# Splitting the first batch's x on GpSimd, another order of the first loads, and g_norm's column on ScalarE's queue

## The chip, the cores and the metric

The kernel runs on one core of one Trainium2 chip. The metric is device time in microseconds (us), the median of several executions. A core has five engines with queues of their own: TensorE (PE in the profile; PEld are its weight loads), VectorE (DVE), ScalarE (ACT), GpSimd (POOL) and SyncE (SP). SP does no arithmetic here and issues most of the transfers; ACT and POOL can issue transfers too. All transfers run on the same 16 DMA engines.

## The reference

Three stages in a row, all in float32. The first is a linear attention without softmax over 8 batches of 576 tokens with 8 heads of 64, followed by a root-mean-square norm with a gain. The other two are two-layer networks with 4608 tokens, 512 features and 2048 hidden units.

```
kv  = einsum('bhsd,bhse->bhde', k, v)
out = einsum('bhsd,bhde->bhse', q, kv)
x   = out / sqrt(mean(out*out, -1) + 1e-6) * g_norm      # to [4608, 512]
h   = x @ w_in;   r = max(h, 0);  x = (r*r) @ w_out      # moe
h   = x @ w_in2;  out = (h*cos(h)) @ w_out2              # moe2
```

## The kernel before, in words

The matmuls of the two networks run in a rounded 32-bit format. Each operand is therefore split into a high part (a cast to the rounded format) and a low part (the operand less the high part), and a product is three matmuls: high by high, high by low, low by high. The weights arrive in 64-bit floating point and are converted on DVE and ACT from integer words (`words` and `value`, L107 to L127; L205 and L206 split the result).

The program has two parts. In the first, the attention and half of the first network's work run interleaved: tokens go in tiles of 512 (`TOK`), hidden units in chunks of 128. `run_chunks` (L811) walks over (tile, chunk) pairs; between the matmuls of a chunk it calls `run_jobs`, which carries out a list of small jobs sorted by a position n counted in chunks. The attention of the eight batches, the conversions of weights and the reloads of x are such jobs. Everything with a position of -1 or less is emitted ahead of the first chunk. In the second part, from 424 us on, the rest of both networks runs as products of seven block matmuls (`run_slots`).

The attention of one batch b works in units (b, p, i): p is one of four column blocks of 128 features (two heads), i one of two halves. First `kv_mm` (L250) multiplies keys and values in five blocks of up to 128 tokens, the fifth of 64, and ACT copies the result into kvx (L272). `att_a` (L279) multiplies a block of queries by it (L289); ACT squares the result into sq (L300) and scales it by gcol, the column of g_norm, into og (L301). `att_b` sums the squares on PE (L315) and takes the reciprocal root on ACT (L320, L322). `att_c` refines it with three DVE operations, L330 to L332, of which the last writes xo; xo has three buffers. For batches 0 and 1, `att_d` splits xo directly into the operands xh and xl of the first two tiles: a cast on ACT (L349) and a subtraction on DVE (L350). Batch 0 gives eight units and, as the first tile ends within the second half of its tokens, twelve pieces: per column block one of 288 columns, one of 224 and one of 64. `att_e` stores xo to DRAM on POOL's queue (L356). `layer_in` (L371) then multiplies x by the first weights; its first two chunks run side by side and walk over the four column blocks in order (L380).

The order of the loads is that in which the program calls them on SP's queue. `load_w` (L151) loads a weight block of 512 KB and `load_kv` (L247) a block of keys and values of 512 KB (256 KB the fifth), `load_q` (L276) a block of queries of 288 KB. Two streams, `w_stream` and `kv_stream`, hold the order within each kind, and `advance` issues the next ones. Ahead of the first jobs the program loads the two halves of g_norm's column, weight blocks one and two, five blocks of keys and values, weight blocks three and four, and three blocks of queries; the fourth is loaded when the first block's buffer is free. Conversions are emitted in the order of the weight blocks.

The order of instructions on each engine isn't just the order of the program. A planner goes over them at build time with modelled durations and puts ready instructions first, so that, for instance, ACT's copies into kvx stand ahead of conversions that the program emits earlier. Waits between engines are set by it as well.

Of the kernel before, what the change touches and what calls it, by code (L numbers as in the profile page):

```python
# [13 lines left out]
ALU = mybir.AluOpType  # L14
# [8 lines left out]
def kernel(  # L23
# [15 lines left out]
    nc = tc.nc  # L39
# [7 lines left out]
    NRAW = 4  # L47
    KVB = 5
# [3 lines left out]
    D = 64  # L52
# [16 lines left out]
    gcol = cpool.tile([P, 1], F32, name="gcol")  # L69
# [26 lines left out]
    def as32(ap):  # L96
        return ap.bitcast(F32)
# [114 lines left out]
    def new_x(t, c):  # L212
        more = dict(bufs=2) if t == 1 and c > 1 else {}
        xs[t, c] = [x_p.tile([P, TOK], F32R, tag=n + "2" * len(more), name=n, **more) for n in ("xh", "xl")]
        return xs[t, c]
# [119 lines left out]
    def att_d(*u):  # L335
        b, p, hf = u
        xo = att[u]
        if b >= NEXACT:
            return
        tok = b * S + hf * HS  # L340
        for t in range(NDIRECT):
            lo, hi = max(tok, t * TOK), min(tok + HS, (t + 1) * TOK)
            if lo >= hi:
                continue
            if (t, p) not in xs:
                new_x(t, p)
            h, l = (x[:, lo - t * TOK:hi - t * TOK] for x in xs[t, p])
            piece = xo[:, lo - tok:hi - tok]
            nc.scalar.copy(out=h, in_=piece)  # L349
            nc.vector.tensor_tensor(out=l, in0=piece, in1=as32(h), op=ALU.subtract)  # L350

    def att_e(*u):
        b, p, i = u
# [381 lines left out]
    w_stream = Stream(load_w, conv_w, w_items)  # L735
# [4 lines left out]
    kv_stream = Stream(load_kv, kv_mm, [(b, c) for b in range(B) for c in range(NSC)])  # L740
# [126 lines left out]
        run_jobs(here)  # L867

    for j in range(2):
        nc.sync.dma_start(out=gcol[j * D:(j + 1) * D, :], in_=g_norm.rearrange("(d o) -> d o", o=1))  # L870
    nc.vector.memset(epsb, EPS)
    nc.scalar.activation(out=zerob, in_=epsb, func=AF.Abs_reciprocal_sqrt)
    nc.vector.memset(zerob, 0.0)
# [1 line left out]
    nc.vector.memset(as32(ones[:]), 0.0)  # L875
    for j in range(2):
        nc.vector.memset(as32(ones[j * D:(j + 1) * D, j * D:(j + 1) * D]), 1.0)
    nc.vector.tensor_scalar(out=gcol, in0=gcol, scalar1=-0.5 / D, scalar2=None, op0=ALU.mult)

    with ExitStack() as early:  # L880
        pools["ps"] = early.enter_context(tc.tile_pool(name="ps0", bufs=1, space=PSUM))
        def right(name, bufs):
            return early.enter_context(tc.tile_pool(name=name, bufs=bufs, side="right"))

        right("pad", 1).tile([P, 56], F32, name="pad")
        ev_p, pools["raw"] = right("ev", 2), right("conv", 2)
        x_p, g_p, pools["t"] = (right(n, b) for n, b in (("x", XB), ("g", 3), ("tmp", 8)))
        with tc.tile_pool(name="att", bufs=1, side="right") as att_p:
            kvx = [att_p.tile([P, NKC, P], F32, tag=f"kvx{b}", name=f"kvx{b}") for b in range(2)]
            for x in kvx:  # L890
                nc.gpsimd.memset(x, 0.0)
            w_stream.advance(2)
            kv_stream.advance(KVB)
            w_stream.advance(NRAW - 2)
            for p in range(NQ):
                load_q(0, p)
            run_jobs(-1)
            banks.update(o=["o", "l1"], ss=["ss"], l=["l0", "acc3"])
            run_chunks(0, nAtt)
        pools["x"] = ctx.enter_context(tc.tile_pool(name="xb", bufs=13, side="left", reuse_waits="tile"))  # L900
        banks["l"] = ["l0", "l1", "o", "ss"]
        run_chunks(nAtt, nA0)
        for c in chunks[-LAG:]:
            layer_out(*c)
# [48 lines left out]
```

## Time and profile before

| | |
|---|---|
| Median of 3 runs | 1560.13 us (1560.1 to 1560.59) |
| The profiled execution's own time | 1560.23 us |
| Its span, from first to last instruction | 1558.5 us |
| PE busy (matmuls) | 1532.7 us |
| DVE busy | 1294.7 us |
| ACT busy | 1076.2 us |
| POOL busy | 108.6 us |
| Moved by DMA | 426.71 MB, mean 274 GB/s |

Times in the profile count from the first instruction of the program. Some 1.7 us of the execution's own time lie around the span. An engine counts as busy while one of its instructions runs; issuing a transfer doesn't count on SP. In a row of the timeline the number in brackets is how long the engine was idle before the instruction, with what ended the idleness. A `q` behind an engine's name stands for its queue's sequencer.

### The profile page before, as it was taken

The page shows a single profiled execution, that of the slowest core. Times are in us where ns is not written, and L with a number is a line of the kernel's source. Part 1 is how long each engine was busy: PE and PEld are TensorE (multiplying, and loading weights), DVE is VectorE, ACT ScalarE, POOL GpSimd, SP SyncE. Part 2 cuts the span into 40 slices and gives each one's busy share as a digit, 9 for nine tenths or more (in the row PEclk, how much of TensorE's full clock was granted, in tenths as well). Part 3 has the DMA queues.
Part 4 walks back from the last instruction along what each step waited for, and adds up shares of the span by engine and source line. Part 5 has one row for each costly group of instructions (what it writes and reads, how often), then busy time and mean ns, then how long its engine had stood idle before and what let it go on. Part 6 is the DMA issues. An engine that isn't in the chain of part 4 may idle for free.

```text
span 1558.5 us, 24657 instructions
## 1 busy us (share of the span) xinstructions
PE 1532.7 (98%) x9104; PEld 1346.8 (86%) x9104; DVE 1294.7 (83%) x1744; ACT 1076.2 (69%) x1529; POOL 108.6 (7%) x172
## 2 busy tenths in 40 slices
PE   5999999999999999999999999999999999999998
PEld 3777777778888888888998899999999999999998
DVE  7987888888886899989889979867986788779777
ACT  5977777775444765656556777776777677777775
POOL 1112111110000000000000000000000000000001
PEclk9999999999999999999999999999999999999999
DMA  9848998777678979898999788887888789899996
GB/s 322 281 148 240 284 284 268 229 214 214 202 230 296 327 246 375 294 382 268 364 340 372 261 281 253 257 280 214 256 248 283 214 246 275 290 336 293 298 314 170
DMA packets 222295, 426.71 MB, mean 274 GB/s; under 512 B 18016, under 2 KB 138080, under 8 KB 222176
## 3 DMA queue, kind: packets, MB, share of 16 engines
q1 hardware_dynamic: 210560, 390.13, 73.4%
q0 software_dynamic: 11616, 35.01, 10.5%
q8 instruction: 73, 1.20, 0.3%
q14 instruction: 46, 0.38, 0.1%
HBM read 317.72 MB, written 81.79 MB: 256 GB/s over the span
## 4 chain that ended last, share of the span: by engine, by line
PE 88%; DMA 4%; DVE 4%; issue 2%; ACT 1%; SPq 0%; POOL 0%; DVEq 0%; ACTq 0%; POOLq 0%
PE FB L506 15%; PE FA L506 15%; PE SA L639 15%; PE SB L639 15%; PE acc L417 12%; PE l L380 10%; DMA ws<-ws_d 1%; PE o L380 1%; PE ss L380 1%; DMA xraw<-x_d 1%; DMA q<-in_qT 1%; DMA sum<-part 1%; DMA wi<-wi_d 1%; PE l L259 1%; DVE gl L616 0%
## 5 line engine op out<-in xcount | busy, mean ns | idle before, releaser
L506 PE MATMUL FA<-xh,wi 128*128 128x512 f32 (+1 forms) x840 | 301.4, 370 | 0.0
L506 PE MATMUL FB<-xh,wi 128*128 128x512 f32 (+1 forms) x840 | 301.4, 370 | 0.0
L639 PE MATMUL SA<-ws,gh 128*128 128x256 f32 x1008 | 233.2, 280 | 0.4 <-issue 0.4
L639 PE MATMUL SB<-ws,gh 128*128 128x256 f32 x1008 | 233.0, 280 | 0.5 <-ACT part L664 0.5
L639 PEld LDWEIGHTS SA<-ws,gh 128*128 128x128 f32 x1008 | 183.7, 188 | 13.0 <-ACT y L558 0.7
L639 PEld LDWEIGHTS SB<-ws,gh 128*128 128x128 f32 x1008 | 183.3, 188 | 12.4 <-ACT part L664 0.7
L506 PEld LDWEIGHTS FB<-xh,wi 128*128 128x128 f32 x840 | 157.2, 188 | 9.4
L506 PEld LDWEIGHTS FA<-xh,wi 128*128 128x128 f32 x840 | 157.1, 188 | 9.0
L639 PE MATMUL SB<-ws,gl 128*128 128x256 f32 x504 | 141.2, 280 | 0.3 <-DVE gl L616 0.3
L639 PE MATMUL SA<-ws,gl 128*128 128x256 f32 x504 | 141.2, 280 | 0.1
L616 DVE TENSOR_TENSOR gl<-y,gh 128x1024 fp32r<-128x1024 f32 (+1 forms) x98 | 109.5, 1117 | 36.5 <-ACT gh L615 36.4
L576 DVE SCALAR_TENSOR_TENSOR y<-y,h 128x1024 f32<-128x1024 f32 (+1 forms) x79 | 88.2, 1117 | 46.2 <-ACT y L572 45.9
L665 POOL DMA_DIRECT2D sum<-part x54 | 46.5, 862 | 1136.3 <-DMA wi_d<-raw 530.3
L558 ACT ACTIVATE y<-h,zerob 128x1024 int32<-128x1024 f32 (+1 forms) x79 | 84.1, 1064 | 49.1 <-DVE h L532 48.5
L417 PE MATMUL acc<-gh,wh 128*128 128x512 f32 x288 | 113.6, 396 | 0.0
L417 PE MATMUL acc<-gl,wh 128*128 128x512 f32 x288 | 112.9, 392 | 0.0
L417 PE MATMUL acc<-gh,wl 128*128 128x512 f32 x288 | 112.6, 391 | 0.0
L506 PE MATMUL FA<-xl,wi 128*128 128x512 f32 (+1 forms) x300 | 110.9, 370 | 0.0
L506 PE MATMUL FB<-xl,wi 128*128 128x512 f32 (+1 forms) x300 | 110.9, 370 | 0.0
L568 ACT ACTIVATE y<-y 128x1024 f32<-128x1024 f32 (+1 forms) x79 | 77.2, 978 | 36.0 <-DVE y L562 36.0
L639 PE MATMUL SA<-gh,ws 128*128 128x512 f32 (+1 forms) x280 | 100.8, 369 | 1.1 <-DMA ws<-ws_d 0.6
L639 PE MATMUL SB<-gh,ws 128*128 128x512 f32 (+1 forms) x280 | 100.6, 369 | 0.1
(181 smaller groups left out, 3816.6 us busy)
## 6 DMA issues: line engine op xcount, KB each, us to landing
wi<-wi_d SPq DMA_DIRECT2D x210, 512.0 KB, 6.6
ws<-ws_d SPq DMA_DIRECT2D x210, 512.0 KB, 5.5
sum<-part POOLq DMA_DIRECT2D x33, 512.0 KB, 7.3
kvld<-in_kv SPq DMA_DIRECT2D x32, 512.0 KB, 6.7
ws_d<-raw SPq DMA_DIRECT2D x24, 448.0 KB, 4.3
q<-in_qT SPq DMA_DIRECT2D x32, 288.0 KB, 4.4
p_d<-ev SPq DMA_DIRECT2D x18, 512.0 KB, 3.7
raw<-in_wA SPq DMA_DIRECT2D x16, 512.0 KB, 6.0
```

What stands on the lines that cost most here:

```text
L259: nc.tensor.matmul(kv_ps[b][r, p, r], t[:n, 0, head], t[:n, 1, head], start=(c == 0 and p == 0), stop=(c == NSC - 1), skip_group_check=True,)
L380: nc.tensor.matmul(ps, a[:, 0, cs], m[:], start=(c == 0 and k == 0), stop=(c == NKC - 1 and k == 2))
L417: nc.tensor.matmul(o, a[:, cs], m[:], start=(f == 0 and n == 0), stop=(f == NH - 1 and n == 2), skip_group_check=True)
L506: nc.tensor.matmul(ps[:, pp, :], a, b, start=(n == 0 and (i in (0, 2) or i == 1 and not seeded(k))), stop=(n == 5), skip_group_check=True,)
L558: nc.scalar.activation(out=y.bitcast(I32), in_=hs[k, b], func=AF.Identity, bias=zerob)
L568: nc.scalar.activation(out=y, in_=y, func=AF.Sin, scale=math.pi)
L576: nc.vector.scalar_tensor_tensor(out=y, in0=y, scalar=-2.0 * math.pi, in1=hs.pop((k, b)), op0=ALU.add, op1=ALU.mult)
L616: nc.vector.tensor_tensor(out=l, in0=src, in1=as32(h), op=ALU.subtract)
L639: nc.tensor.matmul(ps[:, b, :], lhs, rhs, start=(n == 0 and (m == 0 or b % 2 == 0) and i in (0, 1, 2)), stop=(n == 5), skip_group_check=True,)
L665: nc.gpsimd.dma_start(out=e, in_=part, accum_op=ALU.add)
```

## The change

Three edits. The split of batch 0's xo runs on POOL, cast and subtraction; that of batch 1 stays on ACT and DVE. The two loads of g_norm's column are issued on ACT's queue instead of SP's, and its scaling runs on POOL instead of DVE. The third weight block is loaded behind three of the five blocks of keys and values instead of behind all five.

```diff
@@ att_d
             piece = xo[:, lo - tok:hi - tok]
-            nc.scalar.copy(out=h, in_=piece)
-            nc.vector.tensor_tensor(out=l, in0=piece, in1=as32(h), op=ALU.subtract)
+            cast, low = (nc.gpsimd.tensor_copy, nc.gpsimd) if b == 0 else (nc.scalar.copy, nc.vector)
+            cast(out=h, in_=piece)
+            low.tensor_tensor(out=l, in0=piece, in1=as32(h), op=ALU.subtract)
@@ start of the program
     for j in range(2):
-        nc.sync.dma_start(out=gcol[j * D:(j + 1) * D, :], in_=g_norm.rearrange("(d o) -> d o", o=1))
+        nc.scalar.dma_start(out=gcol[j * D:(j + 1) * D, :], in_=g_norm.rearrange("(d o) -> d o", o=1))
...
-    nc.vector.tensor_scalar(out=gcol, in0=gcol, scalar1=-0.5 / D, scalar2=None, op0=ALU.mult)
+    nc.gpsimd.tensor_scalar(out=gcol, in0=gcol, scalar1=-0.5 / D, scalar2=None, op0=ALU.mult)
...
             w_stream.advance(2)
-            kv_stream.advance(KVB)
-            w_stream.advance(NRAW - 2)
+            kv_stream.advance(3)
+            w_stream.advance(1)
+            kv_stream.advance(KVB - 3)
+            w_stream.advance(NRAW - 3)
```

## Rows read from the trace of the kernel before

**Rows 1.** The page, first part: busy time, share of the span, instructions.

```profile
PE 1532.7 (98%) x9104; PEld 1346.8 (86%) x9104; DVE 1294.7 (83%) x1744; ACT 1076.2 (69%) x1529; POOL 108.6 (7%) x172
```

**Rows 2.** Waits of PE, whole span: us in total, times, longest.

```profile
PE o L259 <- DMA kvld<-in_kv: 11.1, 3, 9.3
PE ss L315 <- ACT sq L300: 2.3, 1, 2.3
...
PE acc L315 <- ACT sq L300: 1.5, 1, 1.5
...
PE SA L639 <- DMA ws<-ws_d: 0.6, 1, 0.6
```

**Rows 3.** Timeline, SP's queue: start, us, engine, line, what, count.

```profile
0.74 1.23 SPq L870 DMA_DIRECT2D gcol<-in_g_norm  x2
2.02 1.05 SPq L151 DMA_DIRECT2D raw<-in_wA  x2
...
22.78 2.85 SPq L276 DMA_DIRECT2D q<-in_qT  x3
```

**Rows 4.** DMA issues, stretch 22.7 to 23.2: KB each, us from issue to landing.

```profile
q<-in_qT SPq DMA_DIRECT2D x1, 288.0 KB, 11.7
```

**Rows 5.** Windows: PE, PEld, DVE, ACT, POOL busy; granted clock, DMA share, GB/s.

```profile
3.00:36.00 33.00, 20.13 (x194) 14.09 (x194) 25.03 (x56) 18.86 (x46) 2.98 (x5) 1.00 1.01 356
...
16.68:38.71 22.03, 15.36 (x123) 9.96 (x120) 21.06 (x49) 18.26 (x48) 3.52 (x6) 1.00 1.00 362
...
38.70:42.10 3.40, 3.40 (x9) 2.41 (x9) 2.15 (x6) 2.92 (x9) 0.00 (x0) 0.52 1.00 367
```

**Rows 6.** Timeline, 7 to 21 us, five of its rows.

```profile
7.24 0.72 ACT L112 ACTIVATE e<-e,expb 128x512 int32<-128x512 int32 x1 [5.00 <-DVE e L111]
...
15.81 1.12 PE L259 MATMUL o<-kvld 64*64 64x64 f32 x16 [0.56 <-DMA kvld<-in_kv]
16.68 0.43 DVE L111 TENSOR_SCALAR e<-raw 128x512 uint32<-128x512 uint32 x1 [2.64 <-DMA raw<-in_wA]
...
17.04 0.74 ACT L272 COPY kvx<-o 64x256 f32<-64x256 f32 x2 [3.71 <-PE o L259]
...
18.72 2.26 PE L289 MATMUL acc<-q,kvx 128*128 128x288 f32 x4 [1.79 <-DMA q<-in_qT]
```

**Rows 7.** Timeline, 34.6 to 38.3 us, PE and ACT.

```profile
34.71 1.13 PE L289 MATMUL acc<-q,kvx 128*128 128x288 f32 x4
...
37.10 0.52 ACT L349 CAST xh<-xo 128x224 fp32r<-128x224 f32 x2 [0.71 <-DVE xo L332]
...
37.65 0.41 ACT L300 ACTIVATE sq<-acc 128x288 f32<-128x288 f32 x1
...
38.11 0.51 PE L315 MATMUL ss<-sq,ones 128*128 128x288 f32 x1 [2.28 <-ACT sq L300]
```

**Rows 8.** Timeline, 28 to 35 us: a store and the multiplication behind its landing.

```profile
28.62 0.57 POOL L356 DMA_DIRECT2D x_d<-xo  x1 [1.72 <-DVE xo L332]
...
34.37 0.46 DVE L332 TENSOR_TENSOR xo<-m,og 128x288 f32<-128x288 f32 x1 [0.17 <-DMA x_d<-xo]
```

**Rows 9.** Windows of L349 alone (ACT), then of L350 alone (DVE).

```profile
24.00:45.20 21.20, 4.03 (x12) 0.92 1.00 337
...
24.00:45.20 21.20, 3.91 (x12) 0.92 1.00 337
```

**Rows 10.** Timeline: first cast and last subtraction of batch 0.

```profile
26.13 0.47 ACT L349 CAST xh<-xo 128x288 fp32r<-128x288 f32 x1
...
44.52 0.53 DVE L350 TENSOR_TENSOR xl<-xo,xh 128x224 fp32r<-128x224 f32 x2
```

**Rows 11.** Groups of POOL: whole span (L665, L891), 24 to 45.2 us (L356).

```profile
L665 POOL DMA_DIRECT2D sum<-part x54 | 46.5, 862 | 1136.3 <-DMA wi_d<-raw 530.3 <-ACT part L664 524.7 <-DMA ws<-ws_d 38.5
...
L891 POOL MEMSET kvx<- 128x512 f32 x2 | 1.0, 526 | 0.3 <-POOLq L941 0.3
...
L356 POOL DMA_DIRECT2D x_d<-xo x8 | 4.6, 575 | 38.4 <-DVE xo L332 38.4
```

## The prediction

> **What bounds the kernel now.** I read the page first, for the share of the span in which the matmul engine works: 1532.7 of 1558.5 us [rows 1]. So the end moves by what the 26 us without a matmul lose or win, and by little else. The waits of PE say where these lie [rows 2]: 11.1 us in front of the product of keys and values of batch 0, which waits for loads; 2.3 and 1.5 us in front of the sums of squares (L315), which wait for ScalarE; a wait of the far later L639, for weights, is 0.6 us. All that the change can win lies in the first 45 us; behind them PE is the bound and passes a shift on to the end nearly whole.
>
> What sets the pace of those 45 us I read from the windows [rows 5]. From 3 to 36 us the DMA engines are full (share 1.01, 356 GB/s), so a load lands when the bytes ahead of it have gone: the fourth block of queries is issued at 22.78 and lands 11.7 us later, at 34.48 [rows 3, 4]. From 16.68 to 38.71 VectorE (DVE) is full too: 21.06 of 22.03 us [rows 5]. The timeline then shows the two stops that matter. DVE stands still for 2.64 us until the third weight block is there at 16.68, while it could have converted it [rows 6]. And after the four matmuls of the last column block of batch 0 (34.71, as soon as its queries have landed) PE waits 2.28 us for a square on ScalarE (ACT) at 37.65, which stands in ACT's queue behind a cast of x that itself had waited 0.71 us for DVE [rows 7].
>
> **The change part by part.** *g_norm's column.* SP issues its two loads first, 1.23 us, and the first weight block at 2.02 instead of 0.74 [rows 3]. With them on ACT's queue, all loads of SP start 1.28 us earlier, and with the DMA engines full up to 36 us each lands 1.28 us earlier. On ACT the two issues stand in front of its table load; ACT's next work, at 7.24, comes after 5.00 us of idleness [rows 6], and it moves to 5.96 at the earliest: about 3.7 us of cover for 1.23 us of issues, cost nothing. The scaling of the column moves to GpSimd (POOL) in front of the two memsets of kvx (0.53 us each [rows 11]); kvx is first written at 17.04 [rows 6], so a wait of a few us for the column costs nothing there either.
>
> *Order of loads.* The third weight block goes in front of two blocks of keys. Those land one block later: 512 KB at 356 GB/s [rows 5] are 1.47 us, less the 1.28 gained, so +0.2 us. The matmuls on the last of them start at 15.81, ACT's copies behind them at 17.04 [rows 6]: these stay within 0.2 us, and the first query matmul, at 18.72 now and held by its queries, comes at about 18.1, held by the copies; the queries land at 17.3. The weight block itself lands at 16.7 - 1.28 - (the two blocks of keys, 768 KB, 2.2 us) = 13.2 us. DVE's stop of 2.64 us goes, and with it that much backlog from the queue that is full until 38.71.
>
> *The split of batch 0.* Twelve casts leave ACT (4.03 us in all) and twelve subtractions leave DVE (3.91 us) [rows 9]; three quarters, some 3.0 and 2.9 us, lie ahead of the square at 37.65. Behind the last cast stands no ACT work that waits for DVE any more. Both lists go to POOL, which until then only issues the stores of x_d (eight of 0.575 us, 38.4 us idle in front of them [rows 11]). POOL runs its queue in order, so a unit's store is now queued behind its casts and subtractions, and the next unit's behind that store. Two wait for it: PE's first layer for the split, and DVE for the stores, since a buffer of xo (three of them) is free only when its store has landed. The second store is issued at 28.62, and the multiplication into that buffer starts at 34.37, released by the landing after 0.17 us [rows 8]. This is what is late next: if that unit comes 1.5 us earlier (the first query matmul 0.6 us earlier, and part of DVE's 2.64 us) and four operations of 0.33 us stand in front of its store, the store comes only 0.2 us earlier. DVE's lead then ends in a wait for buffers; but ACT's square no longer hangs on that multiplication, so the end does not. The trace has no cast or subtraction on POOL. Its own rows bound one: from below the memset, 0.53 us for 512 columns, so 0.2 us for the mean piece of 192; from above the longest group on that engine, 0.862 us each (L665) [rows 11]. I take the duration of the same work on its old engines, 0.34 and 0.33 us (4.03 and 3.91 over 12), as the nearest rows: then the split arrives no later than now, cost 0. With the two ends it is -0.3 and +1.1 us for the last cast and subtraction as a pair.
>
> GPSIMD Engine Reference, section 3.1 (Elementwise — side-by-side cycle accounting), of the Trainium skill gives a two-input elementwise operation on GpSimd 1.96 times VectorE's duration; as an estimate the subtractions would then take 0.64 us, inside these bounds. No run here shows it so far.
>
> **The sum.** The place to count is the wait at 38.11. First, the last query block lands 1.28 us earlier, and PE's matmuls on it can start at 33.4 instead of 34.71, since DVE has 2.64 + 2.9 = 5.5 us less in front of it, and PE has the 1.79 us in front of its first query matmul [rows 6] and the 1.5 us of the other unit's sum of squares [rows 2] to give up: **-1.28**. Second, the square needs only the first two of the four matmuls, and ACT no longer waits for DVE in front of it. The wait of 2.28 us then shrinks to something between 0 and the 1.5 us of the same wait on the other unit [rows 2], where no cast stood in front; I take the middle, 0.75: **-1.5**. Third, the clock: from 38.70 to 42.10 the granted clock is 0.52, the lower of its two levels (1.2 of 2.4 GHz), straight after the idle stretch that ends at 38.11 [rows 5, 7]. At the full level that work would take half, 1.7 us less. I take it as staying, because PE idles before 33.4 instead: 0, the other end **-1.7**. Together -2.8 us on the profiled execution's 1560.23 us, 1557.4; the median of the runs shown lies 0.1 us below that execution, so **1557.3 us**. With wait two between its ends and POOL between its own, this case reaches from 1555.8 to 1559.0.
>
> **Rivals.**
>
> *Everything gives.* Both waits go fully and the clock isn't lowered again: -1.28 - 2.28 - 1.7 = -5.3, 1554.9; half of the way there counts as this case, from 1556 down. For it: PE would have no idle stretch of over a us behind the last query block. Against it: the idleness in front of that block grows, since its landing is the DMA engines' and nothing in the change shortens that by more than 1.28.
>
> *VectorE stands still while GpSimd reads.* If a subtraction on DVE and an operation on POOL can't read SBUF together, then moving the split only moves DVE's idleness: 24 operations of 0.33 us are 7.9 us taken from a full queue, against 3.91 us relieved and 2.64 us of the stop, 1.4 us later than now by 45 us. Against the 1.28 us that all loads gain and DVE's own idle us behind 38.71, that is about 0: 1559.9, between 1559 and 1561. For it: nearly everything on DVE in that stretch is full, 21.06 of 22.03 us. Against it: nothing in this trace lets the two meet on tiles. SBUF — State Buffer, section Who interferes with whom, of the Trainium skill states just this rule: a VectorE instruction with two inputs in SBUF and a GpSimd instruction that reads SBUF exclude each other. No row of the trace before can bear it out, as POOL reads no tile there.
>
> *POOL becomes the chain (slower).* The first split starts at 26.13 and the last ends at 45.05 [rows 10], 18.9 us for 24 operations and eight stores. Starting 1.5 us earlier, at 24.6, POOL has 20.4 us before it is later than today; less 4.6 for the stores that is 0.66 us for an operation, twice the 0.33 of its predecessors. Above this point PE's first layer waits for POOL. At the upper bound, 0.862 us, the last split would come at 24.6 + 4.6 + 20.7 = 49.9 instead of 45.05, and the end 4.8 us later: 1565. The stores behind the splits come later from the same point, and DVE's multiplications with them. For it: one engine in order now does what two did. Against it: the pieces are short, and between column blocks POOL waits for DVE anyway.
>
> *The planner.* The order on each engine is drawn up from modelled durations. If it moves the conversions of later weights in front of batch 0's chain, some of the 2.8 us go; that stays within the cases above.
>
> **How the numbers follow.** Forecast 0.47, everything gives 0.20, VectorE stands still 0.18, POOL the chain 0.15. A difference of 0.2%, 3.1 us, is about what can be told from no change here: faster means under 1557.0. Of the forecast's 0.47 about 0.21 lie below that, of the second case 0.20: faster 0.41. Same: 0.26 of the forecast, 0.17 of the third case, 0.02 of the fourth just above its point: 0.45. Slower, above 1563.2: 0.14, the fourth but for that and a rest of the third. The range reaches from the second case's sum, 1554.8, to 1561.6, above the third case and a little into the fourth.
>
> **What would show it.** SP's first weight load at about 0.8 us and DVE's first conversion near 5.5. No stop of DVE for the third weight block. The fourth query block landing near 33.2, and the wait in front of the sum of squares behind it under 1.5 us. The granted clock behind that. POOL's casts and subtractions at 0.2 to 0.66 us each; DVE's subtractions and multiplications of two SBUF tiles still at 0.45 us for 288 columns while POOL works (longer ones speak for the third case). The forecast is wrong if the query block lands as late as now, if PE waits on POOL's output, or if a wait of the same length appears behind 45 us, where batch 1's chain and the conversions share DVE.

## The result and the profile after

The changed kernel takes **1567.95 us** (median of 5 runs, 1566.78 to 1570.44) where the kernel before, run beside it, takes 1560.5 us (5 runs, 1560.1 to 1561.47): ratio 1.0054, interval 1.0043 to 1.0064, slower by about half a per cent. The forecast was 1557.3 us, with a range up to 1561.6. The profiled execution after took 1566.78 us, its span is 1565.0 us, 6.5 us longer than before.

The page's line of busy times, answering to [rows 1]:

```profile
PE 1536.0 (98%) x9104; PEld 1349.1 (86%) x9104; DVE 1297.3 (83%) x1731; ACT 1074.5 (69%) x1517; POOL 122.6 (8%) x197
```

PE does the same matmuls in 3.3 us more, and it is idle for 3.2 us more: span less busy time is 29.0 us against 25.8 us before. So half of the 6.5 us are waits and half are slower matmuls. The waits of PE up to 60 us (us in total, times, longest), answering to [rows 2]:

```profile
PE o L259 <- DMA kvld<-in_kv: 11.9, 3, 8.7
PE l L381 <- POOL xh L350: 5.6, 3, 3.1
PE l L381 <- POOL xl L351: 2.0, 2, 1.3
...
PE acc L315 <- ACT sq L300: 0.6, 1, 0.6
```

The waits for ACT's squares, 3.8 us before, are down to 0.6; in their place PE waits 7.6 us for GpSimd's casts and subtractions, in front of the first layer (lines behind L349 have moved by one: L350 is the cast, L351 the subtraction, L357 the store, L381 the first layer). The slower matmuls are in the windows (columns as in [rows 5]):

```profile
30.08:33.49 3.41, 3.41 (x65) 3.29 (x61) 3.41 (x5) 2.01 (x4) 3.14 (x6) 0.50 1.04 408
33.50:40.30 6.80, 2.92 (x22) 1.42 (x22) 5.15 (x11) 1.46 (x3) 5.14 (x11) 1.00 0.40 157
40.30:47.14 6.84, 5.66 (x12) 4.10 (x13) 2.61 (x3) 3.29 (x8) 1.38 (x3) 0.50 0.28 82
```

The granted clock stands at its lower level (0.50) for 3.4 and 6.8 us, where before there is one such stretch of 3.4 us [rows 5]. In the window before the second one PE worked 2.92 of 6.80 us. At this level PE is busy for 3.41 and 5.66 us, 5.7 us more than before; if half of that would do at the upper level, an estimate, the lower clock makes up some 2.8 of the 3.3 us by which PE's busy time grew.

Groups from 24 to 53.4 us (busy us, mean ns of one, idle before them), first VectorE in the kernel before, then GpSimd and VectorE in the kernel after:

```profile
L331 DVE SCALAR_TENSOR_TENSOR m<-m,r 128x288 f32<-128x288 f32 x10 | 4.5, 454 | 0.1
L332 DVE TENSOR_TENSOR xo<-m,og 128x288 f32<-128x288 f32 x10 | 4.5, 454 | 0.3 <-DMA x_d<-xo 0.2
...
L330 DVE SCALAR_TENSOR_TENSOR m<-acc,r 128x288 f32<-128x288 f32 x6 | 2.7, 454 | 0.0
```

```profile
L351 POOL TENSOR_TENSOR xl<-xo,xh 128x288 fp32r<-128x288 f32 x4 | 3.5, 882 | 0.1
L351 POOL TENSOR_TENSOR xl<-xo,xh 128x224 fp32r<-128x224 f32 x4 | 2.7, 674 | 0.1
L350 POOL CAST xh<-xo 128x64 fp32r<-128x64 f32 x4 | 1.9, 467 | 0.0
L351 POOL TENSOR_TENSOR xl<-xo,xh 128x64 fp32r<-128x64 f32 x4 | 1.8, 446 | 0.0
L350 POOL CAST xh<-xo 128x224 fp32r<-128x224 f32 x4 | 1.8, 444 | 3.0 <-DVE xo L332 3.0
L350 POOL CAST xh<-xo 128x288 fp32r<-128x288 f32 x4 | 1.7, 422 | 24.3 <-DVE xo L332 24.3
```

```profile
L331 DVE SCALAR_TENSOR_TENSOR m<-m,r 128x288 f32<-128x288 f32 x9 | 7.0, 800 | 0.1
L332 DVE TENSOR_TENSOR xo<-m,og 128x288 f32<-128x288 f32 x9 | 5.5, 616 | 1.9 <-DMA x_d<-xo 1.6
L330 DVE SCALAR_TENSOR_TENSOR m<-acc,r 128x288 f32<-128x288 f32 x6 | 2.6, 449 | 0.2 <-ACT r L322 0.2
L125 DVE SCALAR_TENSOR_TENSOR w<-w,e 128x512 f32<-128x512 uint32 x2 | 2.1, 1072 | 0.1
```

The reader is to see two prices here. A subtraction of 288 columns takes 0.88 us on GpSimd on the mean of four (1.11 us once, 0.80 to 0.81 three times). And VectorE's own operations grew: L331 and L332, with two tiles in SBUF, take 0.80 and 0.62 us where the same shapes took 0.454 us before, while L330, whose first input is in PSUM, stays at 0.449 us. One place of the timeline shows the two engines alternating (start, us):

```profile
31.32 2.26 DVE L331 SCALAR_TENSOR_TENSOR m<-m,r 128x288 f32<-128x288 f32 x2
```

```profile
31.50 0.43 POOL L350 CAST xh<-xo 128x288 fp32r<-128x288 f32 x1
...
32.45 0.81 POOL L351 TENSOR_TENSOR xl<-xo,xh 128x288 fp32r<-128x288 f32 x1
```

Two L331, 0.9 us of work, last 2.26 us around a cast and a subtraction of GpSimd (1.24 us together). Then ScalarE's timeline in front of the last square, answering to [rows 7]:

```profile
38.68 0.72 ACT L112 ACTIVATE e<-e,expb 128x512 int32<-128x512 int32 x1 [3.14 <-DVE e L111]
42.29 0.62 ACT L205 CAST wh<-w 128x512 fp32r<-128x512 f32 x1 [2.88 <-DVE w L125]
43.69 0.41 ACT L300 ACTIVATE sq<-acc 128x288 f32<-128x288 f32 x1 [0.79 <-PE acc L289]
```

Two steps of a weight block's conversion stand ahead of the square, and each waits some 3 us for VectorE. In the kernel before, one of them stood ahead of it as well, with hardly a wait:

```profile
35.66 0.72 ACT L112 ACTIVATE e<-e,expb 128x512 int32<-128x512 int32 x1 [0.36 <-DVE e L111]
```

In the kernel after neither holds the square, though: what it waits for last is PE, for 0.79 us. On PE the products with the fourth query block, at 34.71 before [rows 7], now start late, as the first layer's matmuls on the third column block stand ahead of them:

```profile
41.48 0.79 PE L381 MATMUL l<-xl,wh 128*128 128x512 f32 x1 [1.34 <-POOL xl L351]
...
42.50 1.16 PE L289 MATMUL acc<-q,kvx 128*128 128x288 f32 x2
```

At the front, SP's queue and the DMA issues, answering to [rows 3]; ahead of them one issue row of the kernel before, for the column:

```profile
gcol<-in_g_norm SPq DMA_DIRECT2D x2, 0.2 KB, 2.3
```

```profile
gcol<-in_g_norm ACTq DMA_DIRECT2D x2, 0.2 KB, 5.8
```

```profile
0.73 0.87 SPq L151 DMA_DIRECT2D raw<-in_wA  x2
...
6.09 0.97 SPq L247 DMA_DIRECT2D kvld<-in_kv  x2
7.53 0.34 SPq L151 DMA_DIRECT2D raw<-in_wA  x1
```

SP's first load is issued at 0.73 instead of 2.02. But the column, issued beside the large loads, lands after 5.8 us in place of 2.3, at 6.08 and 7.51, and SP's issues at 6.09 and 7.53 each come 0.01 to 0.02 us behind one of these landings: they waited for it, 2.1 and 0.5 us by the trace. SP's first query block is issued at 7.91, before at 8.07: of the 1.29 us won at the first load, 0.16 are left there. The fourth query block lands at 33.87, before at 34.47. That difference says little: in the eight kernels below whose loads and column are as before, it lands between 32.61 and 34.96.

### The profile page after: what moved, and what is told of

It is laid out like the page before. It is cut to its first block, busy times and chain, and to the rows that moved or that the text cites. A ratio compares the mean times of both kernels' runs of the same rounds, so it can differ in the third digit from the quotient of the medians.

```text
span 1565.0 us, 24664 instructions
## 1 busy us (share of the span) xinstructions
PE 1536.0 (98%) x9104; PEld 1349.1 (86%) x9104; DVE 1297.3 (83%) x1731; ACT 1074.5 (69%) x1517; POOL 122.6 (8%) x197
## 4 chain that ended last, share of the span: by engine, by line
PE 90%; DMA 3%; DVE 2%; issue 1%; ACT 1%; POOL 0%; DVEq 0%; POOLq 0%; SPq 0%
PE FB L507 16%; PE FA L507 15%; PE SB L640 15%; PE SA L640 15%; PE acc L418 13%; PE l L381 11%; DMA ws<-ws_d 1%; PE o L381 1%; PE ss L381 1%; DMA sum<-part 1%; DMA wi<-wi_d 1%; PE l L259 1%; PE o L293 0%; PE l L293 0%; PE ss L317 0%
## 5 line engine op out<-in xcount | busy, mean ns | idle before, releaser
L617 DVE TENSOR_TENSOR gl<-y,gh 128x1024 fp32r<-128x1024 f32 (+1 forms) x98 | 109.5, 1118 | 37.4 <-ACT gh L616 37.2
L381 PE MATMUL l<-xh,wh 128*128 128x512 f32 x240 | 96.6, 402 | 6.2 <-POOL xh L350 5.6
L569 ACT ACTIVATE y<-y 128x1024 f32<-128x1024 f32 (+1 forms) x79 | 77.2, 978 | 36.5 <-DVE y L563 36.2
```

What stands on the lines that cost most here:

```text
L381: nc.tensor.matmul(ps, a[:, 0, cs], m[:], start=(c == 0 and k == 0), stop=(c == NKC - 1 and k == 2))
L569: nc.scalar.activation(out=y, in_=y, func=AF.Sin, scale=math.pi)
L617: nc.vector.tensor_tensor(out=l, in0=src, in1=as32(h), op=ALU.subtract)
```

## The experiments

Each ran in five rounds beside the kernel before, whose medians lay at 1559.4 to 1560.0 us; compared is the ratio. e1, e3, e4 and e5 were put on record together, before any of them ran; the others were chosen after seeing the results of earlier ones. One number beside the times turned out to order them: when the last subtraction of batch 0 (its twelfth) ends in the trace.

| run | what | ratio (interval) | last query product starts | last split ends |
|---|---|---|---|---|
| before | | 1 | 34.7 | 45.0 |
| after | all three edits | 1.0054 (1.0043 to 1.0064) | 42.5 | 53.3 |
| e1_split | split alone | 1.0038 (1.0024 to 1.0051) | 39.9 | 50.8 |
| e2_gcol | column alone | 0.9997 (0.9988 to 1.0006) | 35.4 | 44.5 |
| e3_loads | order of loads alone | 1.0017 (1.0008 to 1.0025) | 40.0 | 48.0 |
| e4_no_split | loads and column | 1.0010 (1.0001 to 1.0019) | 37.9 | 45.3 |
| e14_loads_order | loads, PE's order put back | 1.0002 (0.9993 to 1.0010) | 35.5 | 44.6 |
| e9_gcol_only_late | column behind the queries | 1.0011 (1.0002 to 1.0020) | 37.5 | 46.0 |
| e5_after_order | after, PE's order put back | 1.0044 (1.0032 to 1.0057) | 36.2 | 52.1 |
| e10_act_order | e5, and ScalarE's conversion steps held back | 1.0021 (1.0012 to 1.0030) | 36.4 | 48.7 |
| e7_xo_bufs | after, five buffers of xo | 1.0038 (1.0025 to 1.0050) | 41.7 | 52.5 |
| e13_order_bufs | e10, five buffers of xo | 1.0016 (1.0007 to 1.0025) | 36.1 | 47.4 |
| e6_pool_copy | before, split repeated on GpSimd | 1.0050 (1.0037 to 1.0062) | 37.2 | 51.5 |
| e6b_pool_memset | before, GpSimd writes only | 1.0004 (0.9995 to 1.0013) | 35.3 | 44.7 |
| e6c_pool_casts | before, GpSimd casts scratch | 1.0015 (1.0006 to 1.0024) | 36.6 | 48.8 |
| e12_sub_pool | subtractions alone | 1.0028 (1.0016 to 1.0039) | 38.5 | 48.4 |
| e17_sub_order | and both orders of e10 | 1.0037 (1.0024 to 1.0049) | 38.6 | 49.2 |
| e11_cast_pool | casts alone | 1.0049 (1.0036 to 1.0062) | 41.5 | 51.1 |
| e16_cast_order | and both orders of e10 | 1.0018 (1.0009 to 1.0027) | 36.8 | 45.5 |
| e15_late_bufs | a candidate without the split | 1.0016 (1.0007 to 1.0025) | 32.8 | 47.5 |

A straight line through the twenty points gives 0.91 us of time (the ratio's excess times 1560 us) for each us by which the last split ends later, with 0.9 us of scatter. This is a pattern that was found afterwards, and it doesn't show a cause: e16's last split ends only 0.5 us later than before and the kernel is 2.8 us slower, e6c's ends 3.7 us later and the kernel is 2.3 us slower.

**Which edit.** Four kernels: the split alone, the column alone, the order of loads alone, and the two without the split.

```diff
 e1_split: only att_d as in the change
 e2_gcol: only the dma_start of gcol and its tensor_scalar as in the change
 e3_loads: only
-            kv_stream.advance(KVB)
-            w_stream.advance(NRAW - 2)
+            kv_stream.advance(3)
+            w_stream.advance(1)
+            kv_stream.advance(KVB - 3)
+            w_stream.advance(NRAW - 3)
 e4_no_split: the change but for att_d
```

> The split of batch 0 on GpSimd alone; loads and g_norm's column as before. The planner keeps PE's order around the fourth query block here: its four matmuls (L289) come right behind the second column block of the first layer, as before the change. Theory A (GpSimd itself costs: it shuts DVE out while it reads, and its splits come late): 1564 to 1567, most of the change's loss, with DVE's m operations (L331) near 0.8 us as in the changed kernel instead of 0.45. Theory B (the new place of the third column block in PE's queue, ahead of the fourth query block, costs, and GpSimd's slowness alone is hidden): 1559 to 1561.5.

> The third weight block behind three blocks of keys, alone. The planner puts the three matmuls of the third column block ahead of the fourth query block in PE's queue, as in the changed kernel, but the split stays on ACT and DVE. Theory A (GpSimd costs): 1558 to 1561, DVE's stop of 2.6 us gone. Theory B (PE's order costs): 1562 to 1565, with PE waiting over 2 us for the third column block's xh ahead of the fourth query block, and the half clock behind it.

> The changed kernel with the split back on ACT and DVE; PE's order is that of the loads alone, third column block ahead of the fourth query block. Theory A (GpSimd costs): 1557 to 1560.5. Theory B (PE's order costs): 1562 to 1566. Both: the difference to the loads alone is that of g_norm's column, within 1 us.

> The edit of g_norm's column alone (its two loads on ScalarE's queue, its scaling on GpSimd). The prediction's step: all loads 1.28 us earlier, the fourth query block at 33.2 instead of 34.5, 1.0 to 1.5 us faster than the kernel before. Rival (the column, issued behind SP's large loads, lands late and SP's next issues wait for it): the column lands near 6 and 7.5 us, the fourth query block at 33.8 or later, and the time within 0.7 us of the kernel before.

The split alone costs 0.38%, 5.9 us; the loads 0.17%, 2.6 us; the column nothing that can be told. The three sum to 0.52%, the change's own 0.54%; the loads and the column together (e4) cost 0.10%. e1 lies in theory A's range, e3 and e4 between the ranges of the two theories. In e2 the column lands at 6.02 and 7.46, as in the kernel after, and the fourth query block at 33.62, within the scatter named above; the products with it start at 35.38, right behind the second column block's last first-layer matmul (35.15). The time is 0.5 us less, interval 1.9 less to 0.9 more.

e1 says more than its time. Its order on PE is that of the kernel before around the last query products: the third column block stands behind them. So the split's 5.9 us are not the price of that order. PE waits for GpSimd there in front of the second block's matmuls, and VectorE's operations are as long as in the kernel after:

```profile
PE l L381 <- POOL xh L350: 3.7, 1, 3.7
...
PE l L381 <- POOL xl L351: 0.9, 1, 0.9
```

```profile
L331 DVE SCALAR_TENSOR_TENSOR m<-m,r 128x288 f32<-128x288 f32 x10 | 7.9, 801 | 0.1
```

An order still plays into it, VectorE's own: four steps of a weight block's conversion (L206, L111, L113, L116) run from 34.62 to 36.70 ahead of the xo (36.62) whose split PE waits for. No run takes the two apart.

**PE's order.** In the kernel after, as in e3, the planner put the third column block's first-layer matmuls ahead of the last query products. In e5 and e14 they are queued behind them again.

```diff
     def layer_in(t, *fs):
         for c in range(NKC):
+            after = last_q.get(0) if len(fs) > 1 and c == 2 else None
+            with tc.issue_after(after) if after is not None else nullcontext():
                 ...
```

> The changed kernel, all three edits, with the third and fourth column blocks of the first two chunks queued on PE behind the last matmul of batch 0's fourth query block, as PE's order was before the change. Theory A (GpSimd itself costs): at most 2 us better than the changed kernel, 1565 to 1568. Theory B (PE's order costs): 1557 to 1561, the fourth query block's matmuls near 34 to 35 us instead of 42.5, no half clock after 40.

> The order of loads alone, with the third column block of the first two chunks queued on PE behind the last query product of batch 0, as in the kernel before. If PE's order is what the loads' edit costs (1561.9 without this): PE's waits in front of the first layer between 35 and 40 us go, the last query products start by 36 us, and the time is 1559 to 1560.5. If the later kvx copies and VectorE's wait for a store are what it costs: 1561.3 or more.

For the loads this order is the whole cost by the ratios, 1.0017 becomes 1.0002, though their intervals still touch. In e3 PE stops for 1.60 us within the second column block and for 1.53 us in front of the third; in e14 it has done the query products by then, and waits less for the last square than before:

```profile
36.20 0.50 PE L380 MATMUL l<-xl,wh 128*128 128x512 f32 x1 [1.60 <-DVE xl L350]
...
38.46 0.79 PE L380 MATMUL l<-xh,wh 128*128 128x512 f32 x1 [1.53 <-ACT xh L349]
```

```profile
35.48 1.13 PE L289 MATMUL acc<-q,kvx 128*128 128x288 f32 x4
38.37 0.75 PE L316 MATMUL ss<-sq,ones 128*128 128x288 f32 x2 [1.76 <-ACT sq L301]
```

With the split on GpSimd it is not: e5's 1566.8 us lie in theory A's range. Its products start at 36.19 instead of 42.50, and PE then stands still for their squares; the waits of PE and ACT's timeline in e5:

```profile
PE ss L316 <- ACT sq L301: 5.9, 1, 5.9
```

```profile
38.52 0.72 ACT L112 ACTIVATE e<-e,expb 128x512 int32<-128x512 int32 x1 [3.33 <-DVE e L111]
42.12 0.62 ACT L205 CAST wh<-w 128x512 fp32r<-128x512 f32 x1 [2.88 <-DVE w L125]
42.76 0.41 ACT L301 ACTIVATE sq<-acc 128x288 f32<-128x288 f32 x1
```

**ScalarE's order.** e10 also queues ScalarE's steps of the sixth weight block's conversion behind batch 0's last gate. VectorE's steps are not held, though the expectation has both (in e17, with the same edit, VectorE's L111 runs at 34.95, ScalarE's L112 at 45.4). And this is another order than that of the kernel before, where L112 stands ahead of the square too.

```diff
     def conv_w(*item):
+        after = last_og.get(0) if item == ("one", 0, 2, 1) else None
+        with tc.issue_after(after) if after is not None else nullcontext():
             for _ in conv_steps(*item):
                 pass
```

> The kernel after, with PE's third and fourth column block queued behind batch 0's last query product, and ScalarE's and VectorE's part of the sixth weight block's conversion behind batch 0's last gate. Theory C (what costs is conversions queued ahead of the last square, while GpSimd's own price is small): the 5.9 us wait of PE in front of the last sum of squares shrinks under 2.5 us and the time falls to 1561 to 1563. Theory A (GpSimd's price, as the split comes late and VectorE is stretched): the wait moves to the first layer's matmuls, behind GpSimd, and the time stays at 1564.5 or above.

1.0021, or 1562.7 us, in theory C's range. The long wait is gone, and with both orders set 0.33 of the change's 0.54% are gone; most of the waits that are left stand where theory A has them, in front of the first layer. No run gives the kernel before e10's order on ScalarE, so a part of the 0.33 may be a gain that it would have as well. The waits of PE in e10 from 20 to 60 us:

```profile
PE l L397 <- POOL xh L357: 4.2, 3, 2.3
PE l L397 <- POOL xl L358: 1.9, 2, 1.0
```

**Buffers of xo.** In the kernel after VectorE waits 1.61 us for a store's landing, in e10 1.86 us for a subtraction of GpSimd that still reads the buffer.

```diff
-        xo = att_p.tile([P, HS], F32, tag="xo", name="xo", bufs=3)
+        xo = att_p.tile([P, HS], F32, tag="xo", name="xo", bufs=5)
```

> The kernel after with five buffers of xo in place of three; all queues in the order of the kernel after. If the wait of VectorE for a store's landing (1.6 us at 35.57) and for GpSimd's reads of xo carry the loss on, the time falls by 1 to 3 us, to 1564 to 1566.5. If VectorE's stretched operations and GpSimd's own lateness carry it, the freed time is taken up by the next wait and the time stays within 0.8 us of the kernel after (1567.2 to 1568.5).

> The kernel with PE's order and the sixth weight block's conversion put back (1562.7 with three buffers) with five buffers of xo; all queues otherwise in the same order. VectorE's wait of 1.86 us at 35.78 for GpSimd's subtraction to release a buffer, and its 1.10 us at 48.02 for a store, go. If these are the last of the loss: 1560 to 1561.3. If GpSimd's lateness and the stretched operations are: PE's waits for GpSimd's casts and subtractions stay at 5 us or more and the time at 1562 to 1563.

Both waits go (VectorE's idle time in front of L332 is 0.3 and 0.2 us), and the time is 0.16% less in e7 and 0.05% less in e13, with intervals that overlap those of the kernels with three buffers. e7's 1566.0 us lie in the first range of its expectation, e13's 1562.3 in the second, though PE's waits for GpSimd's casts are 3.8 us there and not 5. With the waits gone VectorE's L331 gets longer, 0.88 us on the mean in both: part of the time goes into the next collision.

**Reading at the same time.** These leave the split where it was and give GpSimd work that nobody reads, behind each store of batch 0 (the edits are shortened).

```diff
+            if b == 0:
+                with tc.issue_after(store):
+                    for n in (HS,) if i == 0 else (224, 64):
 e6_pool_copy:
+                        nc.gpsimd.tensor_copy(out=s, in_=source)
+                        nc.gpsimd.tensor_tensor(out=scratch2, in0=source, in1=as32(s), op=ALU.subtract)
 e6b_pool_memset:
+                        nc.gpsimd.memset(scratch[:, :n * 9 // 8], 1.0)
+                        nc.gpsimd.memset(scratch[:, :n * 21 // 8], 1.0)
 e6c_pool_casts:
+                        for k in range(3):
+                            nc.gpsimd.tensor_copy(out=scratch[:, 288:288 + n], in_=scratch[:, :n])
```

> The kernel before, whose real split stays on ScalarE and VectorE; added: GpSimd repeats casts and subtractions of the same sizes on a constant tile into scratch behind each store of batch 0, which nobody reads. Theory A2 (VectorE's operations with two SBUF inputs and GpSimd's reads of SBUF exclude each other): DVE's L331 and L332 lie at 0.6 to 1.0 us instead of 0.45 while GpSimd works, the operation with one PSUM input stays at 0.45, and the time is 1.5 to 4 us above the kernel before, more than in the run with GpSimd's memsets in their place. Rival (the loss is only the split's own lateness on GpSimd): DVE's durations stay at 0.45 us and the time within 1 us of the kernel before.

> As the run with GpSimd's added casts and subtractions, but in their place GpSimd writes constants for about as long, reading nothing. Theory A2 (shared reads): DVE's durations are those of the kernel before, 0.45 us, and the time within 1.2 us of it. If GpSimd's mere activity, its writes, or the later stores cost, this run is as slow as the one with reads.

> The kernel before with GpSimd added work that nobody reads: behind each store of batch 0, three casts of a constant tile into scratch for each piece of x, in place of one cast and one subtraction; these read one tile of SBUF each. The queues of PE, ScalarE and VectorE stand in the order of the kernel before, as they do in the run with memsets. Theory A2 (VectorE's two-tile operations and GpSimd's reads exclude each other): L331, L332 and the subtractions of VectorE become longer than their 0.45 us for 288 columns, 0.55 to 0.9 us on the mean, the operation with a PSUM input stays at 0.45, and the time is 1.0 to 4 us above the run with memsets (1560.3). Rival (the run with repeated splits was slow for its other order alone): durations of 0.45 us, and a time within 0.8 us of the run with memsets.

In e6 the planner drew up another order for VectorE and ScalarE (conversions ahead of batch 0's chain), so its 0.50% can't be put down to reads, and L331 and L332 lie at 0.50 and 0.48 us, below what was expected. In e6b and e6c the queues of PE, ACT and DVE stand as before. VectorE's groups from 24 to 53.4 us, e6b (writes only) and then e6c (reads):

```profile
L332 DVE TENSOR_TENSOR xo<-m,og 128x288 f32<-128x288 f32 x10 | 4.5, 454 | 0.4 <-DMA x_d<-xo 0.3
L331 DVE SCALAR_TENSOR_TENSOR m<-m,r 128x288 f32<-128x288 f32 x10 | 4.5, 453 | 0.1
...
L330 DVE SCALAR_TENSOR_TENSOR m<-acc,r 128x288 f32<-128x288 f32 x6 | 2.7, 453 | 0.0
```

```profile
L331 DVE SCALAR_TENSOR_TENSOR m<-m,r 128x288 f32<-128x288 f32 x9 | 5.0, 555 | 0.1
L332 DVE TENSOR_TENSOR xo<-m,og 128x288 f32<-128x288 f32 x9 | 4.5, 505 | 0.1
L330 DVE SCALAR_TENSOR_TENSOR m<-acc,r 128x288 f32<-128x288 f32 x6 | 2.7, 447 | 0.0
```

Only where GpSimd read did VectorE's operations with two SBUF inputs grow, by 0.10 us (L331) and 0.05 us (L332) on the mean; the one with a PSUM input did not. GpSimd's added work was longer in e6c, 16.9 us with its own waits against 10.1 us, but that is not the reason: in e6b nine of the twenty L331 and L332 ran beside a memset for 0.2 us or more, and all twenty took 0.45 to 0.46 us, where in e6c some beside a cast took 0.67. The mechanism is shown. Its price here, 0.15% against 0.04%, is 1.7 us, and as the intervals overlap, its size is not secured.

**Casts or subtractions.** One half of the split on GpSimd, then the same with both orders of e10.

```diff
 e11_cast_pool, e16_cast_order:
-            nc.scalar.copy(out=h, in_=piece)
+            (nc.gpsimd.tensor_copy if b == 0 else nc.scalar.copy)(out=h, in_=piece)
 e12_sub_pool, e17_sub_order:
-            nc.vector.tensor_tensor(out=l, in0=piece, in1=as32(h), op=ALU.subtract)
+            (nc.gpsimd if b == 0 else nc.vector).tensor_tensor(out=l, in0=piece, in1=as32(h), op=ALU.subtract)
```

> The kernel before with batch 0's subtractions alone on GpSimd, the casts on ScalarE as before. Theory A: 0.8 us for 288 columns on GpSimd, VectorE's two-tile operations stretched to 0.55 to 0.8 us, 2 to 5 us slower than the kernel before. Rival (the casts, or ScalarE's order, are what costs): within 1 us of the kernel before.

> The kernel before with batch 0's casts alone on GpSimd, the subtractions on VectorE. GpSimd's casts take 0.42 us for 288 columns, about as long as ScalarE's, so if only long operations on GpSimd cost, the time is within 1.2 us of the kernel before. If GpSimd's reads stretch VectorE's two-tile operations and its subtractions wait for the casts, L331, L332 and the subtractions lie at 0.5 to 0.7 us on the mean, and the time is 1 to 3.5 us above.

> Batch 0's casts alone on GpSimd, with PE's third column block behind the last query product and the sixth weight block's conversion behind the last gate. If the 7.4 us of the casts alone (without these two) are the order of the queues: PE has no wait over 2.5 us between 26 and 50 us and the time lies at 1559.5 to 1561.5. If GpSimd's reads cost them: 1564 or above.

> Batch 0's subtractions alone on GpSimd, with the same two orders put back. If GpSimd's price proper is in the subtractions (0.8 us for 288 columns, VectorE's L331 at 0.6 us): 1561.5 to 1564, near the whole change with the orders put back (1562.7). If the order was the cost of the subtractions too: 1559.5 to 1561.

The casts alone cost 0.49%, though VectorE's L331 stays at 450 ns and a cast of 288 columns takes 0.63 us; no branch of the expectation had that. With the two orders 0.18% is left: 1562.2 us, between the two ranges of e16's expectation. So most of that run's loss goes with the orders, with the reserve made at e10. The subtractions alone cost 0.28%, in theory A's range, with L331 at 0.63 us; with the two orders it is 0.37%, above both ranges of e17. PE's order had nothing to mend there, as in e12 the third column block stands behind the query products already. In e17 PE waits 2.9 us for a cast on ACT whose xo comes late, and VectorE's own queue has the next conversion (L111, L113, L116) ahead of that xo, which this edit did not touch. The expectation of e17 can't be decided by it.

**The column late, and a candidate.** e9 loads the column by SP behind the query blocks; e15 adds to that the loads' edit, PE's order and five buffers of xo, without the split. (In both, the column's loads and its scaling at the start of the program are taken out.)

```diff
+            for j in range(2):
+                nc.sync.dma_start(out=gcol[j * D:(j + 1) * D, :], in_=g_norm.rearrange("(d o) -> d o", o=1))
+            nc.gpsimd.tensor_scalar(out=gcol, in0=gcol, scalar1=-0.5 / D, scalar2=None, op0=ALU.mult)
             run_jobs(-1)
```

> The kernel before with g_norm's column loaded by SyncE behind batch 0's query blocks and scaled on GpSimd; nothing else. All loads of weights, keys and queries are issued 1.2 us earlier. If the prediction's term holds once the column no longer stands between them: the fourth query block lands near 33.2 us and the time is 0.8 to 1.8 us below the kernel before. If the 1.28 us are taken up by PE's order and by waits on ScalarE: within 0.6 us of it or above.

> A candidate to beat both kernels: the loads' edit, g_norm's column late, PE's order put back, five buffers of xo, the split on ScalarE and VectorE. If the stop of VectorE for the third weight block, the column's place and the wait for a store's landing are each worth something together: 1556.5 to 1558.8. If PE has other waits that end at the same time (ScalarE's last square, the copies of kvx): 1559.3 to 1560.5.

In e9 the fourth query block lands at 31.69, 2.8 us earlier than before, 0.9 us ahead of the scatter named above and more than the prediction asked for, and the kernel is 0.11% slower: the order had changed again, the query products start at 37.5, 5.8 us behind their landing. In e15 they start at 32.78, and then PE waits 5.3 us for the last square (ACT's queue has a conversion that waits for VectorE ahead of it, as in e5); its 1562.4 us lie above both ranges. No kernel tried beats the one before.

## Why the prediction was wrong

*The split at cost 0: the step that failed.* It was to cost nothing, as the engines that it left were full and the one that it went to was empty. Measured alone, it costs 5.9 us. Three things in the step were wrong.

First, the operations' size: 0.34 and 0.33 us were taken, 0.45 and 0.67 us on the mean of twelve are measured (5.4 and 8.0 us in all). That lies inside the bounds, and the mean of both, 0.56 us, below the deciding point of 0.66 us of the slower rival. But the point was worked out as if GpSimd had only to keep up over the whole stretch. It was busy for 17.1 of the 29.4 us from 24 to 53.4 and mostly waited for VectorE in the rest (the last number of busy time in the window's row):

```profile
24.00:53.40 29.40, 21.15 (x132) 14.73 (x131) 22.43 (x38) 17.55 (x44) 17.10 (x32) 0.83 0.71 241
```

What counts is how long one unit takes from xo to its last subtraction, for PE waits for that and the next unit's chain waits for PE. Before, a pair of pieces takes 1.0 us, from the cast at 37.10 [rows 7] to the end of its subtractions at 38.11:

```profile
37.59 0.52 DVE L350 TENSOR_TENSOR xl<-xo,xh 128x224 fp32r<-128x224 f32 x2
```

After, with the store in between, it takes 2.3 us, 34.02 to 36.28:

```profile
34.02 0.55 POOL L350 CAST xh<-xo 128x224 fp32r<-128x224 f32 x2 [0.76 <-DVE xo L332]
34.51 0.57 POOL L357 DMA_DIRECT2D x_d<-xo  x1
35.10 1.18 POOL L351 TENSOR_TENSOR xl<-xo,xh 128x224 fp32r<-128x224 f32 x2
```

The rival "POOL becomes the chain" had the right mark, the end of the last split, with 49.9 us at its upper bound; it came at 53.3, though GpSimd was not full.

Second, "behind the last cast stands no ACT work that waits for DVE any more". There is: L112 and L205 of the sixth weight block, which waited 3.14 and 2.88 us; L112 stood there before as well (35.66). The conversion goes to and fro between the two engines, so freeing ACT of casts that wait for VectorE does not free its queue of VectorE. In the kernel after, PE is later still and hides this wait; e5 shows it as 5.9 us, and e10 that it goes with the order.

Third, the rival "VectorE stands still while GpSimd reads" was true as a mechanism (e6b and e6c), and its time, 1559.9, was too low all the same. It took 7.9 us from VectorE and set against them the 3.91 us of subtractions, the 2.64 us of the stop and the 1.28 us of the loads. Measured after, nine L331 and nine L332 lost 4.6 us ((0.800 - 0.454 + 0.616 - 0.454) x 9), less than it had, yet already more than the 3.91 us that left; and the loss lies on batch 0's chain, not in the queue's slack. SBUF — State Buffer of the Trainium skill (Who interferes with whom), weighed in the prediction, says that a VectorE instruction with two SBUF inputs contends with a GpSimd instruction that reads SBUF, not with one that only writes it, and that one with at most one SBUF input, outside the two-port modes, does not. e6b and e6c agree. GPSIMD Engine Reference of the Trainium skill, section 3.1 (Elementwise — side-by-side cycle accounting), gives 1.96 times VectorE's duration for a two-input operation. Measured is 0.882 against 0.454 us, 1.94 times on the mean, and 1.8 times in the three of four that took 0.80 to 0.81 us.

*The planner: the cause left in a half-sentence.* "That stays within the cases above" was wrong. The planner moved the third column block's matmuls ahead of the last query products with the loads' edit (e3 and the kernel after; not in e1 or e2), and with the split a second step of a conversion ahead of the last square. For the loads that is all of the 2.6 us by the ratios (e3 against e14). With e10's two orders about two thirds of the casts' own cost go (e11 against e16), and 0.33 of the whole change's 0.54%; as ScalarE's order there is not that of the kernel before, these shares may be too high. The split's cost is not PE's order (e1). How it divides into GpSimd's longer units, VectorE's stretched operations and VectorE's order stays open; e17, meant to tell it, had that last order in its way.

*The column, -1.28 us.* SP's first load did move by 1.29 us, but the column's landing went from 3.7 to 7.5 us and SP waited for it twice, so that not "all loads of SP start 1.28 us earlier": the first query block's is issued 0.16 us earlier. And where 2.8 us arrived (e9), the time did not follow: "PE's matmuls on it can start" with its landing is true only while nothing stands ahead of them in PE's queue. Before, 34.71 comes right behind the second column block's last first-layer matmul (34.47), without idle time of PE; in e2 the products come 1.8 us behind the landing.

*The square's wait, -1.5 us.* The waits for squares did go down, from 3.8 to 0.6 us, but not in the way of the sum: the last query products came 7.8 us later, and the waits stand in front of the first layer instead.

*The order of loads.* VectorE's stop for the third weight block went, as predicted: its L111 comes at 12.55 without idle time. The copies into kvx were to stay within 0.2 us and came 0.8 us later (17.82 against 17.04 [rows 6]). In e3, with the column as before, they come at 18.10 and in e2, with the order as before, at 16.57: the order costs 1.1 us there, and the column gives back 0.3 to 0.5 of it where the sum had 1.28. With PE's order kept, the edit is worth nothing either way (e14), so the work that the stop had delayed was not what the end waited for.

*The clock.* It was taken as staying, with a gain as the other bound. The waits moved it the other way: by the estimate above some 2.8 us of the 6.5 are PE at its lower level, which it shows behind a stretch in which it worked 2.92 of 6.80 us. The sum had no bound on that side.

*The case's own range.* From its terms it would reach from 1556.3 us (-1.28 - 2.28 - 0.3) to 1559.2 (-1.28 - 0.78 + 1.1), not from 1555.8 to 1559.0. The measured time lies far outside either.

## What to carry to other kernels

Moving work from a full engine to an idle one pays only if the chain through it gets no longer; ask for the time from a unit's first input to its last output there, not whether the engine can keep up. Where a planner orders the queues, compare each engine's order before and after an edit first, since a change of one engine's work can move another engine's; an edit's price is known only with that order held fixed. And GpSimd work that reads SBUF is paid by VectorE operations with two SBUF inputs, so it belongs beside VectorE work on PSUM, or where VectorE idles.

## What the runs showed of the hardware

The column's loads of 0.2 KB, alone on ACT's queue, landed 5.4 and 6.2 us after their issue beside SP's large loads, and after 2.3 us when they were issued ahead of them. VectorE's L125 (two SBUF inputs of 512 columns) took 1.07 us on the mean of two in place of 0.69. In e7 a single-input L111 of 512 columns, 0.42 us elsewhere, lasted 1.38 us while GpSimd subtracted for 0.80 us, so two inputs may not be the only case. Of GpSimd's four casts of 64 columns two took 0.24 us and two 0.70; the long ones, at 29.35 and 39.53, ran beside VectorE's operations with two SBUF inputs (L122; L116 and L122), so GpSimd seems to wait for VectorE, too.
